# First token block of an MLP run in two halves around the whole second block, with x and a partial x2 kept in DRAM

## The chip, the cores and the metric

The kernel runs on one core of one Trainium2 chip. The metric is device time in microseconds (us) of one execution. A core has TensorE (PE; its weight loads are listed as PEld), VectorE (DVE), ScalarE (ACT), GpSimd (POOL) and the queues SP and POOL, from which transfers (DMA) are issued. Every engine and every queue works through its own instructions in a fixed order and waits on semaphores for the others.

## The reference

Three layers, all in float32, on 8 batches x 576 = 4608 tokens with 512 features:

```python
kv  = einsum('bhsd,bhse->bhde', k, v)            # linear attention, 8 heads of 64
out = einsum('bhsd,bhde->bhse', q, kv)
x   = out / sqrt(mean(out*out) + 1e-6) * g_norm  # laid out as 4608 x 512
h   = x @ w_in                                   # 512 -> 2048
x2  = (h * cos(h)) @ w_out                       # 2048 -> 512, the first MLP
out = (((x2 @ w1) * (x2 @ w2)) @ w3) @ w_out2    # the second MLP
```

## The kernel before

**Precision.** Every matmul operand is split into a high part (ACT, line 110) and a low part (`src - high`, line 112, on DVE or POOL). A product is three matmuls: high x high, high x low, low x high (`three`, line 501).

**Weights.** The weights come in as 8-byte words and are turned into float32 on the chip, chunk by chunk (`Chunk`, line 115). A chunk is 128 x 512 values: one load of 512 KB, one ACT operation (line 136), four DVE operations (lines 137, 138, 141, 144), and then `put`, which for the first MLP is one split: ACT 110 and DVE 112. The first MLP has 32 chunks: `i0` to `i15` for the 16 column blocks of w_in, `u0` to `u15` for the matching row blocks of w_out. Their order is i0, i1, i2, u0, i3, u1, ... i15, u13, u14, u15 (lines 223 to 229). Their words lie in buffers of w_out tiles that are not in use yet (tags `wo8` to `wo15`), and toward the end in the two `stage` buffers. 40 more chunks (w1, w2, w_out2, w3 of the second MLP) are converted one at a time during later blocks and written to DRAM.

**First MLP.** Tokens are cut into 9 blocks of 512, w_in into 16 column blocks, so there are 144 steps n; block t = n // 16 and column block m = n % 16. One step is `emit_h(n)` (12 matmuls of 128x512 into one of two banks `h`), then g = h * cos(h) (`g_first`, `g_rest`: four ACT and three DVE operations in the first block, one DVE operation more and one ACT operation less later on), and two steps behind `emit_w(n)` (12 matmuls into the four banks `acc`). So PE runs h_n, w_(n-2), h_(n+1), w_(n-1), ... At the first step of a block ("swap", line 883) w_(n-2) is put ahead of h_n, since the new x is split into the one buffer `x` (line 489) only after the old block's last h has read it. After the last w of a block the four `acc` banks are copied and stored to the DRAM tensor `x2_all` (lines 541 to 548).

**Conversion in the first block.** Before the loop 4 x 2 chunks are converted and put. Then each of steps 0 to 11 converts and puts two chunks (lines 891 to 893 and 902, 903). While `load["alone"]` holds (through step 15) all low parts go to DVE.

**Attention.** Attention is made in 16 units u of 288 tokens (batch u // 2, half u % 2). Units 0 and 1 are made before the loop. The others are `unit_stage(u, s)`, with stages s = 0 to 10: loads of k, v and q, kv matmuls, out matmuls, mean squares (s = 6), the Newton steps for the reciprocal root (s = 8, ten small DVE operations, one after the other), a round trip through DRAM that spreads it over partitions (`emit_bc`), and the multiplication `emit_x` (s = 10, line 385). Unit u starts at step `windows[u]`: units 2 and 3 at steps 2 and 4, units 4 and 5 at 15 and 20, units 6 and 7 at 31 and 36. Block 1 (tokens 512 to 1023) needs the end of unit 1 and units 2 and 3. Units 2 and 3 issue their DMAs from POOL, all others from SP. The unit's output `o_sb` has three buffers, k and v are loaded into the two `stage` buffers, the spread root into the one buffer `bc`.

**What sets the order.** The functions emit instructions in the order of the code; a scheduler with a simulated timeline then orders each engine's instructions, with the emission order as priority. So an instruction can run earlier than its place in the code where the simulation has a gap for it.

The second MLP follows the first and is not touched by the change.

Of the kernel before, what the change touches and what calls it, by code (L numbers as in the profile page):

```python
# [26 lines left out]
CHUNK = 512  # L27
# [7 lines left out]
def kernel(  # L35
# [18 lines left out]
    nc = tc.nc  # L54
    B, NPAIR, NHALF, _, HALF = qt.shape
# [5 lines left out]
    KD = DM // P  # L61
# [46 lines left out]
    def split(dst, src, lo_engine=None):  # L108

        nc.scalar.activation(dst[:, 0], src, AF.Copy)  # L110
        lo_engine = lo_engine or even(src.shape[-1])
        lo_engine.tensor_tensor(dst[:, 1], src, f32(dst[:, 0]), ALU.subtract)  # L112


    class Chunk:
# [5 lines left out]
        def load(self):  # L121
            if self.tag == "stage":
                self.words = stage([P, CHUNK, 2], I32, f"{self.name}_w")
            else:
# [53 lines left out]
    def put(count):  # L178
        for c in chunks[state["put"]:state["put"] + count]:
            c.put(c.f)  # L180
        state["put"] = min(len(chunks), state["put"] + count)
# [22 lines left out]
            w_out[m] = t  # L204
        return put

    spare = [f"wo{m}" for m in range(8, NM)]
    place = {}

    def add(name, src, put):  # L210
        place[name] = len(chunks) + 1
        chunks.append(Chunk(name, src, spare[0], put))
        spare.append(spare.pop(0))

    def add_pair(m, s):
        nm, put = (("i", put_w_in), ("u", put_w_out))[s]
        if s == 1 and f"wo{m}" in spare:
            spare.remove(f"wo{m}")
            if "stage" not in spare:
                spare.append("stage")  # L220
        add(f"{nm}{m}", w1pair[m, :, 2 * CHUNK * s:2 * CHUNK * (s + 1)], put(m))

    pairs = [(0, 0), (1, 0)]
    for m in range(2, NM):
        pairs += [(m, 0), (m - 2, 1)]
    pairs += [(NM - 2, 1), (NM - 1, 1)]
    for m, i in pairs:
        add_pair(m, i)
# [255 lines left out]
    x_hl = {}  # L484
    x2_d = dram.tile([P, KD, NT], F32, name="x2_all")

    def split_x(t, c, units=None):
        if t not in x_hl:
            x_hl[t] = m1.tile([P, 2, KD, TB], F32R, tag="x", name=f"x_{t}")
        done = 0  # L490
        while done < TB:
            u, s = divmod(t * TB + done, HALF)
            w = min(TB - done, HALF - s)
            if units is None or u in units:
                split(
                    x_hl[t][:, :, c, done:done + w], o_sb[u][:, c, s:s + w],
                    None if t == 0 else nc.vector,
                )
            done += w

    def three(ps, w, x, first, last):
        nc.tensor.matmul(ps, w[0], x[0], start=first, stop=False)  # L502
        nc.tensor.matmul(ps, w[0], x[1], start=False, stop=False)  # L503
        nc.tensor.matmul(ps, w[1], x[0], start=False, stop=last)  # L504

    def emit_h(n):
        t, m = divmod(n, NM)
        ps = ps_h.tile([P, 512], F32, tag="h", name=f"h_{n}")
        w, x = w_in[m], x_hl[t]
        for c in range(KD):  # L510
            three(ps, (w[:, 0, c], w[:, 1, c]), (x[:, 0, c], x[:, 1, c]), c == 0, c == KD - 1)
        h_ps[n] = ps

    def g_first(n):
        u, r = row(f"u_{n}"), row(f"r_{n}")
        nc.scalar.activation(u, h_ps[n], AF.Identity, bias=0.25, scale=INV_2PI)  # L516
        load["vector"] += 1600
        if n < NM:
            nc.scalar.activation(r, u, AF.Identity, bias=ROUND)
            nc.vector.scalar_tensor_tensor(u, r, ROUND, u, ALU.subtract, ALU.subtract)  # L520
        else:
            nc.vector.tensor_scalar(r, u, ROUND, ROUND, ALU.add, ALU.subtract)  # L522
            nc.vector.tensor_tensor(u, r, u, ALU.subtract)  # L523
        return u

    def g_rest(n, u):
        nc.scalar.activation(u, u, AF.Sin, scale=-TWO_PI_DOWN)  # L527
        nc.vector.tensor_tensor(u, u, h_ps.pop(n), ALU.mult)  # L528
        g = m1.tile([P, 2, TB], F32R, tag="g", bufs=2, name=f"g_{n}")
        split(g, u, None if n < NM else nc.vector)  # L530
        g_hl[n] = g

    def emit_w(n):
        t, m = divmod(n, NM)
        g = g_hl.pop(n)
        for j in range(KD):
            if m == 0:
                acc[j] = ps_acc.tile([P, 512], F32, tag=f"acc{j}", name=f"x2_{t}_{j}")
            w = w_out[m][:, :, j * P:(j + 1) * P]
            three(acc[j], (w[:, 0], w[:, 1]), (g[:, 0], g[:, 1]), m == 0, m == NM - 1)  # L540
        if m == NM - 1:
            for j in range(KD):
                s = row(f"x2s_{t}_{j}")
                if j % 2 == 0:
                    nc.scalar.activation(s, acc[j], AF.Copy)
                else:
                    nc.vector.tensor_copy(s, acc[j])
                nc.sync.dma_start(out=x2_d[:, j, t * TB:(t + 1) * TB], in_=s)

# [279 lines left out]
    if True:  # L829
# [39 lines left out]


        NS = NB * NM
        ready = 2
        windows = {}
        for t in range(NB - 1):
            need = min(NU, -(-(t + 2) * TB // HALF))
            new = list(range(ready, need))
            ready = need
            starts = ((2, 4) if t == 0 else (-1, 4)) if len(new) == 2 else (2,)
            for u, s in zip(new, starts):
                windows[u] = t * NM + s  # L880
        for n in range(NS + 2):
            t, m = divmod(n, NM)
            swap = m == 0 and 0 < n < NS
            if swap:
                emit_w(n - 2)
            stages = []
            if n == NM:
# [12 lines left out]
            run(stages, 2)  # L900
            if n < NS:
                if t == 0 and state["put"] < n_first:
                    put(2)
# [4 lines left out]
                if t + 1 < NB and m == NM - 1:  # L908
                    for c in range(2, KD):
                        split_x(t + 1, c)  # L910
            run(stages, 3)
            if 0 < t < NB - 1:
                if m % 2 == 1 and m >= 3 and state["conv"] > state["put"]:
                    put(1)
                if m % 2 == 1 and state["conv"] < state["load"]:
                    convert(1)
                if m % 2 == 1 and m < NM - 3:
                    prefetch(state["load"] + 1)
            if t == NB - 1:
# [178 lines left out]
```

## Time and profile before

| | us |
|---|---|
| three executions | 1854.87, 1558.01, 1563.22 |
| median of the three | 1563.22 |
| the profiled execution, its own time | 1560.76 |
| span of the profiled execution, first to last instruction | 1559.0 |
| PE busy | 1505.4 (97%) |
| DVE busy | 927.3 (59%) |
| ACT busy | 689.2 (44%) |
| POOL busy | 368.5 (24%) |

The span lacks what lies around the first and the last instruction: 1.76 us in this execution. The page divides the span into 40 slices of 39 us and gives each engine's busy share in tenths. A matmul's end is modelled and matmuls overlap, so a PE that is shown as busy need not be issuing at its full pace; the pace is read from the distance between the starts of successive matmuls, or of successive `u<-h` operations on ACT (line 516), each of which marks the end of one h_n.

### The profile page before, as it was taken

The page shows a single profiled execution, that of the slowest core. Times are in us where ns is not written, and L with a number is a line of the kernel's source. Part 1 is how long each engine was busy: PE and PEld are TensorE (multiplying, and loading weights), DVE is VectorE, ACT ScalarE, POOL GpSimd, SP SyncE. Part 2 cuts the span into 40 slices and gives each one's busy share as a digit, 9 for nine tenths or more (in the row PEclk, how much of TensorE's full clock was granted, in tenths as well). Part 3 has the DMA queues.
Part 4 walks back from the last instruction along what each step waited for, and adds up shares of the span by engine and source line. Part 5 has one row for each costly group of instructions (what it writes and reads, how often), then busy time and mean ns, then how long its engine had stood idle before and what let it go on. Part 6 is the DMA issues. An engine that isn't in the chain of part 4 may idle for free.

```text
span 1559.0 us, 20517 instructions
## 1 busy us (share of the span) xinstructions
PE 1505.4 (97%) x7616; PEld 1274.1 (82%) x7616; DVE 927.3 (59%) x1722; ACT 689.2 (44%) x1385; POOL 368.5 (24%) x301
## 2 busy tenths in 40 slices
PE   6778999999999999999999998999999999999998
PEld 5556787787787787877888787999999998998897
DVE  3999567566575666656665547745434456545453
ACT  4656544544445454444533335433333334333331
POOL 1100011011010111101102005464344317444420
PEclk9799999999999999999999999999999999999999
DMA  8633132332323424334112006121112313233312
GB/s 284 204 99 118 66 113 85 124 102 88 124 77 98 140 78 125 105 98 133 63 55 60 37 2 228 41 75 62 58 51 82 108 48 101 89 102 122 122 60 75
DMA packets 79748, 152.06 MB, mean 98 GB/s; under 512 B 11440, under 2 KB 36192, under 8 KB 79648
## 3 DMA queue, kind: packets, MB, share of 16 engines
q1 hardware_dynamic: 78032, 145.98, 28.8%
q0 software_dynamic: 1616, 4.78, 1.0%
q8 instruction: 59, 0.97, 0.2%
q14 instruction: 41, 0.34, 0.1%
HBM read 111.67 MB, written 39.06 MB: 97 GB/s over the span
## 4 chain that ended last, share of the span: by engine, by line
PE 80%; DVE 5%; DMA 5%; issue 4%; POOL 4%; ACT 2%; SPq 0%; ACTq 0%; POOLq 0%; DVEq 0%
PE X L732 11%; PE h L502 8%; PE h L503 8%; PE x L504 8%; PE h L504 8%; PE x L502 8%; PE x L503 8%; PE V L732 5%; PE o L502 4%; PE o L503 4%; PE o L504 4%; PE Y L732 2%; POOL xc L112 2%; DMA x2r<-x_all 2%; PE kv L271 2%
## 5 line engine op out<-in xcount | busy, mean ns | idle before, releaser
L502 PE MATMUL h<-x,w_in 128*128 128x512 f32 x576 | 230.7, 401 | 15.3 <-DVE u L528 14.1
L732 PE MATMUL X<-xc,w 128*128 128x384 f32 x1152 | 230.0, 337 | 7.9 <-ACT s L740 7.1
L503 PE MATMUL h<-x,w_in 128*128 128x512 f32 x576 | 229.2, 398 | 1.8 <-DVE x L112 1.8
L503 PE MATMUL x<-g,w_out 128*128 128x512 f32 x576 | 226.9, 394 | 2.0 <-DVE g L112 2.0
L504 PE MATMUL h<-x,w_in 128*128 128x512 f32 x576 | 228.0, 396 | 0.0
L504 PE MATMUL x<-g,w_out 128*128 128x512 f32 x576 | 227.4, 395 | 0.0
L732 PEld LDWEIGHTS X<-xc,w 128*128 128x128 f32 x1152 | 204.0, 188 | 21.2 <-ACT s L740 11.3
L502 PE MATMUL x<-g,w_out 128*128 128x512 f32 x576 | 213.3, 392 | 0.0
L112 POOL TENSOR_TENSOR xc<-x2r,xc 128x768 fp32r<-128x768 f32 x70 | 134.9, 1934 | 225.7 <-ACT xc L110 225.7
L516 ACT ACTIVATE u<-h 128x512 f32<-128x512 f32 x144 | 86.1, 598 | 172.9 <-PE h L504 163.9
L112 DVE TENSOR_TENSOR g<-u,g 128x512 fp32r<-128x512 f32 x144 | 107.8, 749 | 72.1 <-ACT g L110 71.9
L522 DVE TENSOR_SCALAR r<-u 128x512 f32<-128x512 f32 x128 | 57.9, 452 | 153.7 <-ACT u L516 153.7
L502 PEld LDWEIGHTS h<-x,w_in 128*128 128x128 f32 x576 | 109.5, 190 | 48.6 <-DVE u L528 22.9
L527 ACT ACTIVATE u<-u 128x512 f32<-128x512 f32 x144 | 91.0, 632 | 131.0 <-DVE u L523 123.5
L112 POOL TENSOR_TENSOR qhl<-q,qhl 128x288 fp32r<-128x288 f32 x48 | 40.2, 839 | 416.8 <-ACT qhl L110 415.8
L110 ACT ACTIVATE g<-u 128x512 fp32r<-128x512 f32 x144 | 90.9, 631 | 92.0 <-DVE u L528 73.7
L503 PEld LDWEIGHTS x<-g,w_out 128*128 128x128 f32 x576 | 108.7, 189 | 26.4 <-DVE g L112 2.4
L503 PEld LDWEIGHTS h<-x,w_in 128*128 128x128 f32 x576 | 109.6, 190 | 24.9 <-DVE x L112 2.5
L504 PEld LDWEIGHTS h<-x,w_in 128*128 128x128 f32 x576 | 109.6, 190 | 22.8
L504 PEld LDWEIGHTS x<-g,w_out 128*128 128x128 f32 x576 | 108.8, 189 | 23.4
L502 PEld LDWEIGHTS x<-g,w_out 128*128 128x128 f32 x576 | 107.8, 188 | 23.6
L528 DVE TENSOR_TENSOR u<-u,h 128x512 f32<-128x512 f32 x144 | 98.7, 686 | 47.1 <-ACT u L527 46.7
(174 smaller groups left out, 2535.2 us busy)
## 6 DMA issues: line engine op xcount, KB each, us to landing
x2r<-x_all SPq DMA_DIRECT2D x44, 384.0 KB, 3.5
kvraw<-in_kv_main_dram SPq DMA_DIRECT2D x28, 512.0 KB, 3.6
x_all<-x2s SPq DMA_DIRECT2D x36, 256.0 KB, 2.1
part<-o SPq DMA_DIRECT2D x36, 256.0 KB, 2.0
part<-part SPq DMA_DIRECT2D x36, 256.0 KB, 2.6
out_dram<-part SPq DMA_DIRECT2D x36, 256.0 KB, 2.8
i_w<-in_w1pair_dram SPq DMA_DIRECT2D x16, 512.0 KB, 5.6
u_w<-in_w1pair_dram SPq DMA_DIRECT2D x16, 512.0 KB, 4.0
```

The costliest lines, as they stand in the source:

```text
L110: nc.scalar.activation(dst[:, 0], src, AF.Copy)
L112: lo_engine.tensor_tensor(dst[:, 1], src, f32(dst[:, 0]), ALU.subtract)
L271: nc.tensor.matmul(ps[d, 0:D], k[:, d], v[:, d], start=i == 0, stop=i == NC)
L502: nc.tensor.matmul(ps, w[0], x[0], start=first, stop=False)
L503: nc.tensor.matmul(ps, w[0], x[1], start=False, stop=False)
L504: nc.tensor.matmul(ps, w[1], x[0], start=False, stop=last)
L516: nc.scalar.activation(u, h_ps[n], AF.Identity, bias=0.25, scale=INV_2PI)
L522: nc.vector.tensor_scalar(r, u, ROUND, ROUND, ALU.add, ALU.subtract)
L527: nc.scalar.activation(u, u, AF.Sin, scale=-TWO_PI_DOWN)
L528: nc.vector.tensor_tensor(u, u, h_ps.pop(n), ALU.mult)
L732: nc.tensor.matmul(ps, w[:, self.i, a, k], x[:, b, k], start=first and k == 0 and n == 0, stop=last and k == 1 and n == 2, skip_group_chec ...
```

## The change

The order of the steps is written out as a list `steps` of (t, m, first, last): first column blocks 0 to 7 of block 0 (n = 0 to 7), then all 16 of block 1 (n = 8 to 23), then column blocks 8 to 15 of block 0 (n = 24 to 31), then blocks 2 to 8 as before. Since block 0 is left and taken up again:

- `save_x0`: two DMAs on SP write units 0 and 1 as far as they belong to block 0 to DRAM ahead of the loop. `load_halves("x0")` at n = 20 loads them into the two `stage` buffers, and `split_x` splits them a second time at the end of step 23 (four splits of 128x512).
- After column block 7 of block 0 the four `acc` banks are copied and stored to a DRAM tensor `part0` (the same copies and stores as at a block's end). They are loaded at n = 28 into the `stage` buffers, and after n = 31's w they are added to the banks by four DVE operations, which take the place of two ACT and two DVE copies.
- There is one swap more: at n = 8, 24 and 32 instead of 16 and 32.
- The 32 first chunks are converted more slowly: at step n so many that 9 + n + min(n, 8) // 2 are done. That is 1, 1, 2, 1, 2, 1, 2, 1 in steps 0 to 7, 2 in step 8, 1 each in steps 9 to 19. The buffers of their words no longer include `stage`; the last chunk's words use the buffer `bc`.
- Units 2 and 3 are no longer placed by `windows`; the table `quick` puts their stages into steps 0 to 6: Newton of unit 2 in step 4, of unit 3 in step 5, `emit_x` in steps 5 and 6. Unit 6 starts at step 33 instead of 31.
- `load["alone"]` holds through step 23, the three-operation DVE form of g through step 31; the low part of g is always on DVE, as it was.
- The 40 later chunks are converted in steps 35 to 127, up to seven a block; before, steps 16 to 127, six a block.

The core of the diff:

```diff
+    HM = NM // 2
+    steps = [(0, m, m == 0, m == HM - 1) for m in range(HM)]
+    steps += [(1, m, m == 0, m == NM - 1) for m in range(NM)]
+    steps += [(0, m, m == HM, m == NM - 1) for m in range(HM, NM)]
+    steps += [(t, m, m == 0, m == NM - 1) for t in range(2, NB) for m in range(NM)]
+    x0_d = dram.tile([P, KD, TB], F32, name="x0")
+    part0_d = dram.tile([P, KD, TB], F32, name="part0")
+    halfway = {}
+    def save_x0():
+        for u in range(2):
+            w = min(HALF, TB - HALF * u)
+            nc.sync.dma_start(
+                out=x0_d[:, :, HALF * u:HALF * u + w], in_=o_sb[u][:, :, 0:w]
+            )
+    def load_halves(name, src):
+        halfway[name] = []
+        for i in range(2):
+            t = stage([P, 2, TB], F32, f"{name}_{i}")
+            nc.sync.dma_start(out=t, in_=src[:, 2 * i:2 * i + 2])
+            halfway[name] += [t[:, k] for k in range(2)]
     def split_x(t, c, units=None):
+        if "x0" in halfway and t == 0:
+            if c == 0:
+                x_hl[t] = m1.tile([P, 2, KD, TB], F32R, tag="x", name=f"x_{t}_again")
+            split(x_hl[t][:, :, c], halfway["x0"][c], nc.vector)
+            return
...
-        if m == NM - 1:
+        if last:
             for j in range(KD):
-                s = row(f"x2s_{t}_{j}")
-                if j % 2 == 0:
+                s = row(f"x2s_{n}_{j}")
+                if m == NM - 1 and t == 0:
+                    nc.vector.tensor_tensor(s, acc[j], halfway["part0"][j], ALU.add)
+                elif j % 2 == 0:
                     nc.scalar.activation(s, acc[j], AF.Copy)
                 else:
                     nc.vector.tensor_copy(s, acc[j])
-                nc.sync.dma_start(out=x2_d[:, j, t * TB:(t + 1) * TB], in_=s)
+                dst = part0_d[:, j] if m < NM - 1 else x2_d[:, j, t * TB:(t + 1) * TB]
+                nc.sync.dma_start(out=dst, in_=s)
...
-            starts = ((2, 4) if t == 0 else (-1, 4)) if len(new) == 2 else (2,)
+            starts = ((1, 4) if t == 2 else (-1, 4)) if len(new) == 2 else (2,)
...
+        quick = {
+            0: [(2, 0), (2, 1), (2, 2)], 1: [(2, 3), (2, 4), (3, 0), (3, 1)],
+            2: [(2, 5), (2, 6), (3, 2)], 3: [(3, 3), (3, 4)], 4: [(2, 8), (3, 5), (3, 6)],
+            5: [(2, 10), (3, 8)], 6: [(3, 10)],
+        }
+        save_x0()
         for n in range(NS + 2):
-            t, m = divmod(n, NM)
-            swap = m == 0 and 0 < n < NS
+            t, m, first, last = steps[n] if n < NS else (NB, n - NS, False, False)
+            swap = first and 0 < n
...
+            more = min(n_first, 9 + n + min(n, 8) // 2) - state["conv"] if n < NS else 0
...
-                if t == 0 and state["conv"] < n_first:
+                if more > 0:
                     prefetch(min(state["conv"] + 8, n_first))
-                    convert(2)
+                    convert(more)
...
-                if t + 1 < NB and m == NM - 1:
+                after = steps[n + 1][0] if last and n + 1 < NS else t
+                if after != t:
                     for c in range(2):
-                        split_x(t + 1, c)
+                        split_x(after, c)
...
+            for u, s in quick.get(n, ()):
+                one = [unit_stage(u, s)]
+                for i in range(4):
+                    run(one, i)
+            if n == NM + 4:
+                load_halves("x0", x0_d)
+            if n == 2 * NM - 4:
+                load_halves("part0", part0_d)
-            if 0 < t < NB - 1:
+            if 2 * NM + 2 < n < NS - NM:
```

## Rows read from the trace of the kernel before

**Rows 1.** The page: span, and busy tenths or granted clock in 40 slices.
```profile
span 1559.0 us, 20517 instructions
PE   6778999999999999999999998999999999999998
DVE  3999567566575666656665547745434456545453
PEclk9799999999999999999999999999999999999999
```
**Rows 2.** Stretches: length, each engine's busy us (count); then clock, DMA share, GB/s.
```profile
35.00:158.00 123.00, 99.93 (x514) 76.17 (x515) 115.79 (x256) 80.74 (x155) 11.21 (x18) 0.90 0.46 148
...
63.40:158.80 95.40, 77.56 (x335) 58.38 (x335) 87.93 (x189) 61.95 (x112) 9.05 (x14) 0.93 0.40 123
158.80:280.60 121.80, 121.80 (x584) 95.83 (x584) 74.79 (x155) 58.67 (x127) 14.68 (x16) 1.00 0.27 84
```
**Rows 3.** Timeline of ACT, chosen h_n ends: n = 0, 7, 8, 13, 33, 94, 95.
```profile
63.41 0.60 ACT L516 ACTIVATE u<-h 128x512 f32<-128x512 f32 x1 [0.85 <-PE h L504]
...
121.06 0.60 ACT L516 ACTIVATE u<-h 128x512 f32<-128x512 f32 x1
126.57 0.58 ACT L516 ACTIVATE u<-h 128x512 f32<-128x512 f32 x1
...
158.85 0.60 ACT L516 ACTIVATE u<-h 128x512 f32<-128x512 f32 x1 [1.21 <-PE h L504]
...
280.62 0.60 ACT L516 ACTIVATE u<-h 128x512 f32<-128x512 f32 x1 [1.21 <-PE h L504]
...
650.82 0.60 ACT L516 ACTIVATE u<-h 128x512 f32<-128x512 f32 x1 [1.58 <-PE h L504]
656.32 0.60 ACT L516 ACTIVATE u<-h 128x512 f32<-128x512 f32 x1 [0.98 <-PE h L504]
```
**Rows 4.** Waits of PE, 63.4 to 158.8 us: total, times, longest.
```profile
PE h L502 <- DVE u L528: 12.3, 9, 2.3
```
**Rows 5.** Timeline of DVE: one conversion's operations and g; two 288-wide operations.
```profile
141.75 0.70 DVE L141 SCALAR_TENSOR_TENSOR i_f<-i_w,i_f 128x512 int32<-128x512 int32 x1
142.35 0.43 DVE L138 TENSOR_SCALAR u_f<-u_f 128x512 int32<-128x512 int32 x1
142.69 0.70 DVE L112 TENSOR_TENSOR g<-u,g 128x512 fp32r<-128x512 f32 x1
143.29 0.70 DVE L144 SCALAR_TENSOR_TENSOR i_f<-i_w,i_f 128x512 int32<-128x512 int32 x1
...
50.98 0.45 DVE L112 TENSOR_TENSOR x<-o,x 128x288 fp32r<-128x288 f32 x1
51.34 0.68 DVE L112 TENSOR_TENSOR w_in<-i_f,w_in 128x512 fp32r<-128x512 f32 x1
```
**Rows 6.** DVE groups, 0 to 126.6 us, shapes apart: last conversion operation of each chunk.
```profile
L144 DVE SCALAR_TENSOR_TENSOR i_f<-i_w,i_f 128x512 int32<-128x512 int32 x13 | 8.9, 686 | 0.0
L144 DVE SCALAR_TENSOR_TENSOR u_f<-u_w,u_f 128x512 int32<-128x512 int32 x11 | 7.6, 687 | 0.0
```
**Rows 7.** Timeline of DVE: the low part of g_6.
```profile
121.81 0.70 DVE L112 TENSOR_TENSOR g<-u,g 128x512 fp32r<-128x512 f32 x1
```
**Rows 8.** Chain of waits, in time: kv matmuls of one head pair.
```profile
154.85 0.95 PE kv L271 x20
```
**Rows 9.** Timelines: unit 3's first and last Newton step, its bc transfers, its emit_x.
```profile
82.38 0.17 DVE L351 TENSOR_SCALAR rs<-rsx 128x18 int32<-128x18 int32 x1
...
101.14 0.18 DVE L357 SCALAR_TENSOR_TENSOR rs<-rs,rs 128x18 f32<-128x18 f32 x1
...
105.67 1.23 POOL L379 DMA_DIRECT2D bc<-rsd  x2 [3.49 <-DVE o L385]
...
110.77 1.19 DVE L385 TENSOR_TENSOR o<-o,bc 128x288 f32<-128x288 f32 x3 [0.51 <-DMA bc<-rsd]
...
113.08 0.45 DVE L385 TENSOR_TENSOR o<-o,bc 128x288 f32<-128x288 f32 x1
```
**Rows 10.** DMA issues: count, KB each, median us from issue to landing.
```profile
kvraw<-in_kv_main_dram SPq DMA_DIRECT2D x28, 512.0 KB, 3.6
x_all<-x2s SPq DMA_DIRECT2D x36, 256.0 KB, 2.1
```
**Rows 11.** Timeline of PE at half clock: two successive matmuls.
```profile
74.06 0.63 PE L502 MATMUL h<-x,w_in 128*128 128x512 f32 x1
74.48 0.63 PE L503 MATMUL h<-x,w_in 128*128 128x512 f32 x1
```

More of the change, by code (lines that the diff above doesn't have):

```diff
@@ L123, in load @@
                 self.words = stage([P, CHUNK, 2], I32, f"{self.name}_w")
+            elif self.tag == "bc":
+                self.words = ap.tile([P, CHUNK, 2], I32, tag="bc", name=f"{self.name}_w")
             else:
@@ L205, in put_w_out, with first_pairs @@
         return put
[L207 to L228, printed above, removed]
+    def first_pairs():
+        pairs = [(0, 0), (1, 0)]
+        for m in range(2, NM):
+            pairs += [(m, 0), (m - 2, 1)]
+        pairs += [(NM - 2, 1), (NM - 1, 1)]
+        free = list(range(NM // 2, NM))
+        for m, s in pairs:
+            if s == 1 and m in free:
+                free.remove(m)
+            tag = f"wo{free[0]}" if free else "bc"
+            free = free[1:] + free[:1]
+            nm, put = (("i", put_w_in), ("u", put_w_out))[s]
+            src = w1pair[m, :, 2 * CHUNK * s:2 * CHUNK * (s + 1)]
+            chunks.append(Chunk(f"{nm}{m}", src, tag, put(m)))
+    first_pairs()
     n_first = len(chunks)
@@ L506, in emit_h @@
     def emit_h(n):
-        t, m = divmod(n, NM)
+        t, m, _, _ = steps[n]
         ps = ps_h.tile([P, 512], F32, tag="h", name=f"h_{n}")
@@ L517, in g_first @@
         load["vector"] += 1600
-        if n < NM:
+        if n < 2 * NM:
             nc.scalar.activation(r, u, AF.Identity, bias=ROUND)
@@ L529, in g_rest @@
         g = m1.tile([P, 2, TB], F32R, tag="g", bufs=2, name=f"g_{n}")
-        split(g, u, None if n < NM else nc.vector)
+        split(g, u, nc.vector)
         g_hl[n] = g
     def emit_w(n):
-        t, m = divmod(n, NM)
+        t, m, first, last = steps[n]
         g = g_hl.pop(n)
         for j in range(KD):
-            if m == 0:
-                acc[j] = ps_acc.tile([P, 512], F32, tag=f"acc{j}", name=f"x2_{t}_{j}")
+            if first:
+                acc[j] = ps_acc.tile([P, 512], F32, tag=f"acc{j}", name=f"x2_{n}_{j}")
             w = w_out[m][:, :, j * P:(j + 1) * P]
-            three(acc[j], (w[:, 0], w[:, 1]), (g[:, 0], g[:, 1]), m == 0, m == NM - 1)
-        if m == NM - 1:
+            three(acc[j], (w[:, 0], w[:, 1]), (g[:, 0], g[:, 1]), first, last)
+        if last:
             for j in range(KD):
-                s = row(f"x2s_{t}_{j}")
-                if j % 2 == 0:
+                s = row(f"x2s_{n}_{j}")
+                if m == NM - 1 and t == 0:
+                    nc.vector.tensor_tensor(s, acc[j], halfway["part0"][j], ALU.add)
+                elif j % 2 == 0:
                     nc.scalar.activation(s, acc[j], AF.Copy)
@@ L871 @@
         NS = NB * NM
-        ready = 2
+        ready = 4
         windows = {}
-        for t in range(NB - 1):
+        for t in range(1, NB - 1):
             need = min(NU, -(-(t + 2) * TB // HALF))
@@ L886 @@
             stages = []
-            if n == NM:
+            if n == NM + HM:
                 load["alone"] = False
+            more = min(n_first, 9 + n + min(n, 8) // 2) - state["conv"] if n < NS else 0
             if n < NS:
                 stages = [unit_stage(u, n - w) for u, w in windows.items() if 0 <= n - w <= LAST]
-                if t == 0 and state["conv"] < n_first:
+                if more > 0:
                     prefetch(min(state["conv"] + 8, n_first))
-                    convert(2)
+                    convert(more)
                 emit_h(n)
@@ L901 @@
             if n < NS:
-                if t == 0 and state["put"] < n_first:
-                    put(2)
-                if t + 1 < NB and m == NM - 1:
+                if more > 0:
+                    put(more)
+                after = steps[n + 1][0] if last and n + 1 < NS else t
+                if after != t:
                     for c in range(2):
-                        split_x(t + 1, c)
+                        split_x(after, c)
                 g_rest(n, uu)
-                if t + 1 < NB and m == NM - 1:
+                if after != t:
                     for c in range(2, KD):
-                        split_x(t + 1, c)
+                        split_x(after, c)
             run(stages, 3)
-            if 0 < t < NB - 1:
+            for u, s in quick.get(n, ()):
[7 more added lines that the diff above has]
+            if 2 * NM + 2 < n < NS - NM:
                 if m % 2 == 1 and m >= 3 and state["conv"] > state["put"]:
@@ L916 @@
                     convert(1)
-                if m % 2 == 1 and m < NM - 3:
+                if m % 2 == 1 and m < NM - 2:
                     prefetch(state["load"] + 1)
+            if n == NS - NM:
+                assert state["put"] == len(chunks)
             if t == NB - 1:
```

1 line of the change is left out of this document (removed).

## The prediction

> **What bounds the kernel now.** The page comes first. PE is at nine tenths in nearly every slice but the first four, which hold the first 156 us; there DVE is the busiest engine and the granted clock dips [rows 1]. So the change can only win in the start, and the question is which engine sets the pace there. The stretches answer it: from 35 to 158 us DVE is busy for 115.8 of 123.0 us, PE for 99.9; from 158.8 to 280.6 us PE is busy for all of 121.8 us and DVE for 61% [rows 2]. The ends of the h matmuls date the change from one regime to the other. In the settled part a step takes 656.32 - 650.82 = 5.50 us, which is 24 matmuls at 0.229 us, or 2.75 us for one h or one w ("half-step"). From the end of h_13 at 158.85 to that of h_33 at 280.62 there are 20 steps in 121.77 us; 20 x 5.495 = 109.9, and the 11.9 us left are the matmuls of units 4 and 5, so nothing is lost after h_13. From h_0's end at 63.41 to h_13's at 158.85 PE did 13 h and 11 w, 24 half-steps, worth 65.9 us, in 95.4 us [rows 3]. With some 4 us of attention matmuls about 25 us are lost there. What PE waits for in that stretch is mostly DVE's product u * h, which frees the bank for the next h (12.3 us, 9 times) [rows 4].
>
> These 25 us are the ceiling of any gain. PE's idle time alone, 95.4 - 77.6 = 17.8 us [rows 2], would put it lower; I take the pace, since the matmuls shown as busy stand further apart there.
>
> The Trainium skill says the same in "Trainium Kernel Development and Optimization", section "Performance Expectations": matmul busy time is a bad metric because matmuls are pipelined, and the weight loads' busy share is a good one. The trace agrees: that share is 61% (58.4 of 95.4 us) against 79% (95.8 of 121.8 us) in the next stretch [rows 2]. By the busy rows the best case below would end near 1543 us instead of 1537.
>
> **What a conversion costs DVE.** By the distance of successive starts, an operation with two tensor inputs over 512 columns costs 0.60 us (141.75 to 142.35), one with a single input 0.34 us (142.35 to 142.69), one over 288 columns 0.36 us [rows 5]. A chunk is two of line 137/138, lines 141 and 144 and the low part of its split: 2 x 0.34 + 3 x 0.60 = 2.48 us. g costs three of 0.60, 1.80 us. So a step with two chunks wants 4.96 + 1.80 = 6.76 us of DVE and PE 5.50 us: DVE leads for the twelve converting steps. A step with one chunk wants 4.28 us and leaves PE in the lead.
>
> **Does DVE work in emission order?** By h_8's end at 126.57 us 13 + 11 = 24 chunks were converted [rows 3, 6]; the code has emitted 8 + 2 x 8 = 24 by the end of step 7. So conversions keep to the code's order, and I can count forward.
>
> **When h_8 ends after the change.** h_8 is now the first h of block 1. By the new schedule 19 chunks are done by the end of step 7, five fewer: 126.57 - 5 x 2.48 = 114.2 us. Added in front of it is the split of x for block 1: four column groups in pieces of 64, 288 and 160 columns, about 0.12 + 0.36 + 0.22 = 0.70 us a group (an estimate that runs a line through the 288 and 512 column prices), 2.8 us in all: 117.0 us. The other route is by w: the swap now puts w_6 ahead of h_8, and w_6 needs the low part of g_6, at 121.81 + 0.60 before [rows 7]. It stands behind the conversions of step 6, of which there are 18 instead of 22: 122.4 - 4 x 2.48 = 112.5 us, then w_6 and h_8, 5.5 us: 118.0 us. Both must hold, so I take 118.0. From below, PE's own pace bounds it: 63.41 plus 8 h and 7 w (41.2 us) plus some 3.5 us of units 2 and 3 is 108 us [rows 3].
>
> **What that is worth.** At 118.0 us PE has done 9 h and 7 w, 16 half-steps. Before, at 158.85 us, it had done 14 h and 11 w, 25, and two head pairs of unit 4, about 1.9 us at 0.95 each [rows 8]. If PE then runs at its pace it needs 9 x 2.75 + 1.9 = 26.6 us to get there: 144.6 instead of 158.85, a gain of **14.2 us**.
>
> **What goes off that.**
> - Step 8 still converts two chunks, and the first g in block 1 comes from a DVE that has no lead: 6.76 - 5.50, say 1.3 us lost. Steps 9 to 19 want 4.28 us of 5.50, so they hide.
> - Moved conversions (13 x 2.48 = 32 us of DVE) less the six later chunks that leave block 1 (11 us), plus four x splits, two copies and four adds (10 x 0.60) come to 27 us; DVE in that stretch goes from 74.8 to about 102 of 121.8 us [rows 2], 84%. Hidden behind PE; if that cover were gone each us would cost one.
> - The swap more: at the swaps at 16 and 32 PE has no idle time, since the whole stretch is busy [rows 2]. Nothing.
> - The DMAs: two saves, two loads of x, four stores and two loads of part0, all on SP. The nearest row has 2.1 us for a store of 256 KB, 3.6 for a load of 512 KB [rows 10]; issue at steps 20 and 28 leaves three and five steps (16 and 27 us). Hidden. The save of unit 0 holds its o buffer, which unit 3 wants, for a few us; the out matmuls of unit 3 come later than that. What waits behind part0 on `stage` is unit 6's first k and v load, 3.6 us, issued only when the adds are done; the kv matmuls that PE meets in the next step may wait. From 0 to 3 us; I take 1.0, since the scheduler can put the next w ahead of them.
> - Seven later chunks a block instead of six are 2.5 us of DVE in 96 us: nothing.
>
> 14.2 - 1.3 - 1.0 = 11.9. The profiled execution took 1560.76 us, 1.76 more than its span and 2.5 less than the median of the runs. 1560.8 - 11.9 = **1549 us**.
>
> **The rivals.**
> 1. *The gate moves to unit 3 (slower).* Before, units 2 and 3 were first wanted at h_16, far behind; now x of block 1 waits for them at h_8. Unit 3's Newton steps ran from 82.4 to 101.3 us, 19 us for ten operations of 0.17 us, since DVE puts others between them; then 9.5 us of round trips to the first emit_x at 110.8, the last ending at 113.5 [rows 9]. That is just in time for 118. But Newton is emitted in step 5, and if DVE takes it only when the step's other work is done (about 100 us; before, it ran far ahead of its place), the same 19 + 9.5 + 2.8 + 2.8 us lead to 134, and h_8 ends near 136. The price is 18 us, at half clock (0.43 us a matmul instead of 0.23 [rows 11]) up to 20: 1567 to 1569 us. It turns the sign when unit 3's last emit_x ends later than about 125 us. For it: every hop is a chain of waits. Against it: in the trace Newton ran well ahead of its place, and its priority is now higher. Chance 0.14.
> 2. *A smaller version, or DVE still leads in block 1.* The twelve x pieces have to fit behind h_7 (one x buffer) on a full DVE, and at 84% with static order some steps of block 1 can wait. Five to ten us go: h_8 near 125, or 1 us lost in each of eight steps. 1554 to 1560, about 1556 us. Chance 0.26.
> 3. *PE's own pace.* If the units' work fills gaps and clock dips go with the stalls, h_8 ends at 108 us, 10 us earlier, and nothing of the 2.3 us is lost: a gain of 24, 1537 us. For it: 5 chunks fewer also shorten PE's wait for banks. Against it: DVE stays full up to h_8. Chance 0.12.
>
> **How the numbers follow.** The forecast has 0.48, with its own range of 1542 to 1555 (h_8 between 112 and 122 us, deductions between 1 and 4 us). The range 1537 to 1562 takes in rival 2 and nearly all of rival 3; left out are most of rival 1 and a little beyond the ceiling, about 0.17. Two per cent of the median, 31 us, is about what a measurement of this kernel can tell from no change. The ceiling of 25 us lies inside it, so faster by more than that needs something that no row shows (0.03); slower by more needs rival 1 at nearly triple price (0.03); within it 0.94.
>
> **What would show it.** In the profile after: h_8's end near 118 us and PE without idle time from there (right), or h_8 late with the waits of its splits on unit 3's emit_x or bc (rival 1), or DVE over 95% busy up to 200 us with PE still waiting for u * h (rival 2). 19 conversions before h_8 shows that the emission order was kept. PE idle around h_24, h_32 or the first kv of unit 6 would show that the reloads are not hidden. The forecast is wrong at its root if the conversions run ahead of the new schedule again, since then DVE is as full before h_8 as it was.

## The result, and the profile after

The changed kernel takes 1546.2 us, median of five runs (1541.4 to 1548.3); the kernel before, run beside it, takes 1559.7. The ratio is 0.991, with a 95% interval of 0.988 to 0.994; one execution of the kernel before took 1854.9 us and is not in it. That is within 2%, 2.8 us under the 1549 forecast and inside the forecast's own range. (1.1 of these 2.8 us come from the base: the forecast started from 1560.8, the kernel before now has 1559.7.) The profiled execution has a span of 1544.4 us, 14.6 less than before [rows 1].

The page of the changed kernel: span, and busy tenths or granted clock in 40 slices.
```profile
span 1544.4 us, 20537 instructions
PE   6799999999999999999999998999999999999998
...
DVE  3998844566566666766666447644544456545453
...
PEclk9799999999999999999999999999999999999999
```
The kernel differs where the forecast looked for it: DVE is at eight tenths in slices 4 and 5 and at four in 6 and 7, where it was at nine, five, six and seven before. The ends of the h matmuls date the change. After, timeline of ACT: the ends of h_0, h_7, h_8, h_12, h_13 and h_33 (start, us; line 516 before is 543 now).
```profile
63.35 0.61 ACT L543 ACTIVATE u<-h 128x512 f32<-128x512 f32 x1
...
109.89 0.60 ACT L543 ACTIVATE u<-h 128x512 f32<-128x512 f32 x1
124.68 0.60 ACT L543 ACTIVATE u<-h 128x512 f32<-128x512 f32 x1 [1.36 <-PE h L531]
...
151.07 0.60 ACT L543 ACTIVATE u<-h 128x512 f32<-128x512 f32 x1 [0.37 <-PE h L531]
156.56 0.60 ACT L543 ACTIVATE u<-h 128x512 f32<-128x512 f32 x1 [1.16 <-PE h L531]
...
266.37 0.60 ACT L543 ACTIVATE u<-h 128x512 f32<-128x512 f32 x1 [0.29 <-PE h L531]
```
h_33 ends at 266.37 us instead of 280.62 [rows 3]: 14.25 us, so the whole gain is made by then. About 1.2 us of it are only moved: unit 6 starts two steps later. Before, 65 kv matmuls are shown from 158.85 to 280.62 us, 25 more than units 4 and 5 still had, and 25 x 0.95 / 20 = 1.2 us [rows 8]. h_143, far behind, ends at 920.51 instead of 933.80 us: 13.3. From h_12 on a step takes 5.49 us, (266.37 - 151.07) / 21, with nothing between: the matmuls of units 4 and 5, which stood after h_13 before, are already done. Stretches of the kernel after: length, busy us (count) of PE, PEld, DVE, ACT and POOL; then clock, DMA share, GB/s.
```profile
63.35:151.07 87.72, 79.75 (x389) 58.47 (x389) 76.68 (x177) 63.16 (x138) 16.83 (x21) 0.92 0.53 154
151.07:266.37 115.30, 115.30 (x505) 94.63 (x504) 71.50 (x133) 64.24 (x116) 7.45 (x8) 1.00 0.14 43
...
125.00:160.00 35.00, 33.97 (x158) 25.31 (x157) 30.60 (x67) 28.06 (x58) 5.71 (x6) 1.00 0.45 132
160.00:260.00 100.00, 100.00 (x439) 82.05 (x438) 59.76 (x106) 55.02 (x102) 7.45 (x8) 1.00 0.15 44
```
PE's idle time before the settled part is 87.72 - 79.75 = 8.0 us; before it was 17.8 [rows 2], so 9.9 us went there. Some 3 us more are matmuls that stand closer together: the work of PE's 77.6 us before [rows 2], with one step less (5.5) and units 4 and 5 more (11.9 - 1.2), would be 82.8 us, and 79.75 are shown. Of PE's wait for u * h, 12.3 us before [rows 4], 1.9 are left. After, waits of PE from 63 to 160 us (total, times, longest):
```profile
PE out L310 <- ACT qhl L110: 2.9, 1, 2.9
PE h L529 <- DVE u L555: 1.9, 3, 1.4
```

### The profile page after: what moved, and what is told of

Read it like the earlier page. It is cut to its first block, busy times and chain, and to the rows that moved or that the text cites. A ratio compares the mean times of both kernels' runs of the same rounds, so it can differ in the third digit from the quotient of the medians.

```text
span 1544.4 us, 20537 instructions
## 1 busy us (share of the span) xinstructions
PE 1500.9 (97%) x7616; PEld 1272.0 (82%) x7616; DVE 924.8 (60%) x1714; ACT 697.5 (45%) x1405; POOL 371.4 (24%) x301
## 4 chain that ended last, share of the span: by engine, by line
PE 81%; DMA 5%; DVE 3%; POOL 3%; ACT 2%; issue 2%; SPq 0%; ACTq 0%; POOLq 0%; DVEq 0%
PE X L762 11%; PE h L529 8%; PE x L531 8%; PE x L530 8%; PE h L531 8%; PE h L530 8%; PE x L529 8%; PE V L762 5%; PE o L529 4%; PE o L530 4%; PE o L531 4%; PE Y L762 3%; POOL xc L112 2%; DMA x2r<-x_all 2%; PE kv L269 1%
## 5 line engine op out<-in xcount | busy, mean ns | idle before, releaser
L529 PE MATMUL h<-x,w_in 128*128 128x512 f32 x544 | 216.3, 398 | 5.1 <-DVE u L555 3.4
L530 PE MATMUL h<-x,w_in 128*128 128x512 f32 x544 | 215.1, 395 | 1.8 <-DVE x L112 1.8
L531 PE MATMUL h<-x,w_in 128*128 128x512 f32 x544 | 215.0, 395 | 0.0
L554 ACT ACTIVATE u<-u 128x512 f32<-128x512 f32 x144 | 91.0, 632 | 121.6 <-DVE u L550 106.7
L112 DVE TENSOR_TENSOR g<-u,g 128x512 fp32r<-128x512 f32 x144 | 104.4, 725 | 64.6 <-ACT g L110 64.4
L110 ACT ACTIVATE g<-u 128x512 fp32r<-128x512 f32 x144 | 90.9, 632 | 109.1 <-DVE u L555 86.3
L529 PEld LDWEIGHTS h<-x,w_in 128*128 128x128 f32 x544 | 103.1, 190 | 33.0 <-DVE u L555 8.0
L531 PEld LDWEIGHTS x<-g,w_out 128*128 128x128 f32 x576 | 108.8, 189 | 23.0
L549 DVE TENSOR_SCALAR r<-u 128x512 f32<-128x512 f32 x112 | 50.7, 453 | 127.3 <-ACT u L543 127.2
L770 ACT ACTIVATE s<-X 128x384 f32<-128x384 f32 x144 | 65.9, 487 | 133.6 <-PE X L762 133.2
L530 PEld LDWEIGHTS h<-x,w_in 128*128 128x128 f32 x544 | 103.1, 190 | 24.4 <-DVE x L112 2.5
```

The lines of the kernel that those rows point to most:

```text
L770: nc.scalar.activation(s, ps, AF.Copy)
```

## The experiments

Three theories could give 14 us. **D**, the prediction's: fewer conversions before h_8 unload DVE, and the block order only makes that permissible. **G**: units 4 and 5 now run in PE's gaps before h_12. Their k and v load earlier, since the words of late chunks no longer take the `stage` buffers. **O**: the block order does something by itself. Later runs ask a second question: what holds h_8 at 124.7 us, the conversions or unit 3's chain. Runs on one chip are compared with each other; the ratio is to the kernel before on the same chip, with its 95% interval.

| run | median us | ratio (95%) | end of h_8 | end of h_33 |
|---|---|---|---|---|
| `stage` again for words | 1545.0 | 0.991 (0.990 to 0.993) | 120.7 | 266.5 |
| before, `stage` kept free | 1555.0 | 0.999 (0.998 to 1.000) | 125.5 | 278.6 |
| two chunks a step | 1558.6 | 1.001 (0.9995 to 1.002) | 130.9 | 276.7 |
| Newton first | 1546.9 | 0.993 (0.991 to 0.994) | 124.6 | 267.0 |
| one chunk a step | 1542.5 | 0.990 (0.989 to 0.992) | 117.1 | 260.4 |
| w_out's low parts on POOL | 1553.2 | 0.996 (0.995 to 0.998) | 133.5 | 273.1 |
| no clamp | 1547.1 | 0.993 (0.992 to 0.995) | 128.4 | 269.0 |
| one Newton round | 1547.8 | 0.993 (0.992 to 0.994) | 120.3 | 263.7 |
| no clamp, one Newton round | 1539.2 | 0.987 (0.985 to 0.989) | 117.8 | 259.1 |
| changed kernel again | 1546.0 | 0.992 (0.990 to 0.993) | 123.5 | 264.6 |
| one chunk a step again | 1541.7 | 0.989 (0.987 to 0.990) | 117.6 | 260.8 |

Rows 1 to 4 ran on one chip, 5 to 7 on a second and 8 to 11 on a third.

**Units 4 and 5 back in their place.** The changed kernel, with the words of late chunks in `stage` again:
```diff
                 free.remove(m)
-            tag = f"wo{free[0]}" if free else "bc"
+                if "stage" not in free:
+                    free.append("stage")
+            tag = free[0] if free[0] == "stage" else f"wo{free[0]}"
```


> The changed kernel with one part undone: words of the late first chunks go into the stage buffers again, as in the kernel before, instead of the buffer bc. In the program this moves the k/v matmuls of batch 2 (units 4 and 5) from steps 2 to 7 back to steps 14 to 20, and all out and mean-square matmuls of units 4 and 5 behind step 17; the conversion schedule and the order of the blocks stay. Theory G (the gain is units 4 and 5's matmuls done in PE's gaps of the first 150 us, let in by the free stage buffers): h_33 ends 8 to 12 us later than in the changed kernel (274 to 278 us), total 1553 to 1557 us. Theory D (the gain is the slower conversion, which frees DVE and brings h_8 forward): h_8 ends earlier or equal, total within 2 us of the changed kernel, 1544 to 1548 us.

The k and v matmuls of units 4 and 5 went back behind h_13, to steps 14 to 20. Stretches of this run, from h_0 to h_13, its part from h_8 on, and from h_13 to h_33, columns as above:
```profile
63.44:145.78 82.34, 74.15 (x294) 57.39 (x294) 75.31 (x168) 56.36 (x112) 8.59 (x13) 0.90 0.38 114
...
120.70:145.78 25.08, 25.08 (x111) 20.61 (x110) 23.23 (x44) 18.51 (x34) 0.00 (x0) 1.00 0.41 130
...
145.78:266.48 120.70, 120.70 (x599) 96.11 (x599) 71.43 (x142) 71.68 (x145) 13.52 (x16) 1.00 0.24 74
```
h_13 ends 10.8 us earlier than in the changed kernel, and the units' work then comes after it: h_33 ends at 266.48 against 266.37, and the time is the same. G falls. This run is also the prediction's own premise, units 4 and 5 behind block 1's first steps, so its terms are read from this run below.

**The same buffers in the kernel before.** Words never in `stage`, the last chunk's in `bc`:
```diff
...
             spare.remove(f"wo{m}")
-            if "stage" not in spare:
-                spare.append("stage")
+            if not spare:
+                spare.append("bc")
```


> The kernel before with one part of the change alone: the words of the first chunks never use the stage buffers, the last chunk's words use bc. Block order and conversion schedule are those of before. In the program the k/v matmuls of batch 2 now stand in steps 1 to 17 instead of 12 to 19, unit 5 stays behind step 22. Theory G: a part of unit 4's matmuls falls into the gaps, 2 to 5 us gained, 1555 to 1558 us. Theory D: no change within 1.5 us of the kernel before.

0.999, with an interval that just holds 1; the median is 2.3 us under that of the kernel before. The units' matmuls come earlier there too. By the interval they buy 0 to 3 us. That doesn't tell the two theories' numbers for this run apart, but it is far from 14.

**The new block order with the old conversions.** The changed kernel with two chunks in each of steps 0 to 11:
```diff
-            more = min(n_first, 9 + n + min(n, 8) // 2) - state["conv"] if n < NS else 0
+            more = min(n_first, 10 + 2 * n) - state["conv"] if n < NS else 0
```


> The changed kernel with the conversion schedule of before: two chunks in each of steps 0 to 11, so 24 instead of 19 before h_8. Units 4 and 5 stay in steps 2 to 10 in the program. Theory D: h_8 ends 5 x 2.48 = 12 us later (near 137 us) and steps 8 to 11 stay short of DVE time; total 8 to 12 us more, 1554 to 1558 us. Theory G: the same total of DVE work is done by step 20 either way, the gaps still take the units; total 0 to 4 us more, 1546 to 1550 us.

The whole gain goes: 1.001. h_7 ends at 120.8 us, as before (121.06 [rows 3]), and h_8 at 130.9. So O falls and D stands: the order of the blocks is worth nothing without the slower conversions.

The opposite half was not run: slower conversions in the old block order. By the order of the chunks, step n needs the first 2n of them. With 8 done ahead of the loop, 1.5 a step would be in time up to step 16 (8 + 1.5 x 16 = 32). By the prices of the prediction such a step wants 1.5 x 2.48 + 1.80 = 5.5 us of DVE, as much as PE takes; this is an estimate. So the runs show that the gain comes from the slower conversions; that it needs the new order of blocks as well they don't show.

**One chunk a step.** The other way on the same scale: 16 chunks by the end of step 7 instead of 19, one in each step but step 8 (two).
```diff
-            more = min(n_first, 9 + n + min(n, 8) // 2) - state["conv"] if n < NS else 0
+            more = min(n_first, 9 + n + (n >= 8)) - state["conv"] if n < NS else 0
```


> The changed kernel with a still slower conversion: one chunk a step (two in step 8), so 16 instead of 19 chunks before h_8, and the last in step 22 instead of 19. Theory D (DVE's conversions ahead of h_8 set its time): three chunks less are 7.4 us of DVE; h_8 near 117 instead of 124.7 us, steps 9 to 22 want 4.3 us of DVE and stay in PE's pace; total 4 to 7 us less than the changed kernel, 1539 to 1542 us. Theory T (only the sum of DVE work up to the end of the conversions counts, and it is the same): total within 1.5 us of the changed kernel.

Run again beside the changed kernel on one chip:

> The kernel with one chunk a step once more, beside the changed kernel on one chip. If fewer conversions ahead of h_8 are worth time: h_8 near 117 us again and the median 2 to 6 us under the changed kernel's. If only the sum of the work counts: within 1.5 us of it.

> The changed kernel once more, unchanged, for comparison on the same chip: ratio to the kernel before 0.990 to 0.992, h_8 within 3 us of 124.7 us.

1541.7 against 1546.0: 4.3 us, with intervals that don't touch. h_8 ends at 117.6 against 123.5, h_33 at 260.8 against 264.6. This version beats both kernels; its gain over before is 1.0% and 1.1% in the two runs.

**What holds h_8 at 124.7?** The timeline of DVE of the changed kernel from 112 us, some lines left out (start, us):
```profile
112.69 0.68 DVE L143 SCALAR_TENSOR_TENSOR i_f<-i_w,i_f 128x512 int32<-128x512 int32 x1
113.30 0.58 DVE L112 TENSOR_TENSOR x<-o,x 128x64 fp32r<-128x64 f32 x2
113.80 0.68 DVE L112 TENSOR_TENSOR w_out<-u_f,w_out 128x512 fp32r<-128x512 f32 x1
114.40 0.72 DVE L112 TENSOR_TENSOR x<-o,x 128x64 fp32r<-128x64 f32 x3
115.04 0.68 DVE L146 SCALAR_TENSOR_TENSOR i_f<-i_w,i_f 128x512 int32<-128x512 int32 x1
115.64 0.45 DVE L112 TENSOR_TENSOR x<-o,x 128x288 fp32r<-128x288 f32 x1
116.01 1.55 DVE L383 TENSOR_TENSOR o<-o,bc 128x288 f32<-128x288 f32 x4
117.49 0.68 DVE L112 TENSOR_TENSOR g<-u,g 128x512 fp32r<-128x512 f32 x1
...
120.24 1.02 DVE L112 TENSOR_TENSOR x<-o,x 128x160 fp32r<-128x160 f32 x4
```
The low part of g_6 (117.49), which w_6 needs, stands behind the 19th chunk, eight of x's pieces and unit 3's emit_x (116.01); x's last pieces, which h_8 needs, stand behind that emit_x too. DVE has no idle time in these lines, so the order alone doesn't tell which of the two gates, the amount of DVE work or unit 3's chain, holds h_8. The next runs take away one, the other, and both.

*Less DVE work:* line 139, the clamp, left out of the first chunks.
```diff
-            yield nc.vector.tensor_scalar(self.f, self.f, MOST, LEAST, ALU.min, ALU.max)
+            if not self.name[0] in "iu":
+                nc.vector.tensor_scalar(self.f, self.f, MOST, LEAST, ALU.min, ALU.max)
+            yield
```


> The changed kernel without the clamp (line 139 of the changed kernel, one DVE operation of 0.34 us a chunk) in the 32 first chunks; the values of these weights that lie outside the clamp's limits are left as they are. DVE does 32 x 0.34 = 10.9 us less, 6.5 us of it before h_8. If a microsecond of DVE work in the start is a microsecond of time: h_8 5 to 7 us earlier and total 6 to 10 us less, 1536 to 1540 us. If PE's order and its waits on the x splits set the time instead: under 3 us.

h_7 ends at 103.77 instead of 109.89: 6.1 us, which is 18 chunks by the 0.34 us of [rows 5] (5.1 us against the repeat of the changed kernel, where h_7 ends at 108.84). But the time is 0.993, no better than the changed kernel. Unit 3's emit_x starts at 117.01, 1 us later than in the changed kernel's profile, DVE now waits for its bc, and x's last pieces start at 120.20, where they did before. No clamp, timeline of DVE:
```profile
117.01 1.70 DVE L385 TENSOR_TENSOR o<-o,bc 128x288 f32<-128x288 f32 x4 [1.07 <-DMA bc<-rsd]
...
120.20 1.03 DVE L112 TENSOR_TENSOR x<-o,x 128x160 fp32r<-128x160 f32 x4
121.15 0.69 DVE L112 TENSOR_TENSOR w_in<-i_f,w_in 128x512 fp32r<-128x512 f32 x1
129.69 0.69 DVE L549 SCALAR_TENSOR_TENSOR u<-r,u 128x512 f32<-128x512 f32 x1 [7.86 <-ACT r L548]
```
DVE then stands idle for 7.9 us: the time won is waited away. (h_8 is listed later, at 128.4, since h_9's matmuls ran among its own; h_9 ends at 130.1 here and at 130.8 in the changed kernel.)

*A shorter chain:* one Newton round instead of three for units 2 and 3.
```diff
...
-        newton(x, y, t)
+        newton(x, y, t, 1 if u in (2, 3) else 3)
```


> The changed kernel with one Newton iteration instead of three in units 2 and 3 (six of the ten small DVE operations left out; the reciprocal roots of these 576 tokens are coarser). Giving Newton priority had not shortened it (86 to 105 us still), so this takes the operations away: unit 3's chain should be some 10 us shorter, its emit_x end near 106 instead of 117.6 us. If unit 3's chain is the gate of h_8 in the changed kernel: h_8 near 118 instead of 124.7 us and the total 4 to 6 us under the repeat of the changed kernel. If DVE's conversions are the gate: h_8 moves by under 2 us and the total by under 2 us.

The first operation of emit_x in this run, timeline of DVE:
```profile
106.50 0.83 DVE L383 TENSOR_TENSOR o<-o,bc 128x288 f32<-128x288 f32 x2 [3.12 <-DMA bc<-rsd]
```
It starts 8.4 us earlier than in the changed kernel's repeat on this chip (114.86), and h_8 ends at 120.3 instead of 123.5. Only 0.9 us of that is left at h_33, and the time is 1547.8 against 1546.0: no gain.

*Both:*

> The changed kernel without the clamp in the 32 first chunks and with one Newton iteration instead of three in units 2 and 3. Without the clamp alone h_7 ended 6.1 us earlier (103.8), as 18 x 0.34 us of DVE less would have it, but h_8 ended at 128.4 us, since unit 3's emit_x came at 117.0 to 118.7 us. If that run's h_8 was held by unit 3's chain: emit_x now ends near 107 us, h_8 near 116 us, total 6 to 10 us under the changed kernel's repeat. If h_8 is held by something else (PE's order, the x buffer): h_8 stays above 123 us and the total within 3 us of it.

1539.2 against 1546.0: 6.8 us. emit_x of unit 3 and h_8 in this run (timelines of DVE and ACT):
```profile
108.86 1.55 DVE L385 TENSOR_TENSOR o<-o,bc 128x288 f32<-128x288 f32 x4
...
117.78 0.60 ACT L545 ACTIVATE u<-h 128x512 f32<-128x512 f32 x1 [0.94 <-PE h L533]
```
Either gate alone is worth nothing and the two together 6.8 us, as two gates that stand side by side would have it.

One rival is not taken apart from this: the granted clock differs too. Stretches of this run and then of the changed kernel's repeat, columns as above:
```profile
45.00:80.00 35.00, 31.40 (x169) 23.02 (x166) 29.45 (x65) 25.34 (x59) 5.52 (x10) 1.00 0.63 199
...
45.00:80.00 35.00, 25.35 (x122) 16.54 (x119) 30.40 (x73) 23.36 (x53) 6.50 (x9) 0.76 0.62 199
```
All five executions of the run with both show a mean granted clock of 0.996 to 0.999 over the whole span, those of the repeat 0.992, so a part of the 6.8 us can be the clock's. Two things speak against its being the whole: h_0 ends 2.4 us earlier here (59.6 against 62.0), but h_7 at 108.4 against 108.8, so that little of the early lead is left there; and the run with one chunk a step, which relieves both gates too, gains 4.3 us with the same 0.76 from 45 to 80 us.

Two gates also fit what one chunk a step gains. It takes three chunks (7.4 us) out of DVE before h_8 and, with fewer conversions between the Newton steps, lets unit 3's Newton take its last step at 93.9 us instead of 105.5. One chunk a step, the run repeated, timeline of DVE:
```profile
93.91 0.17 DVE L355 SCALAR_TENSOR_TENSOR rs<-rs,rs 128x18 f32<-128x18 f32 x1
105.52 1.56 DVE L383 TENSOR_TENSOR o<-o,bc 128x288 f32<-128x288 f32 x4 [4.00 <-DMA bc<-rsd]
```

**Newton first.** The chain shortened without leaving anything out, by priority:
```diff
-            late.append(lambda: emit_newton(u))
+            late.append(lambda: newton_first(u))
...
+    def newton_first(u):
+        with tc.high_priority() if u in (2, 3) else nullcontext():
+            emit_newton(u)
```


> The changed kernel with one wait shortened: the ten Newton steps of units 2 and 3 get priority over all other DVE work, so that they follow each other. In the changed kernel unit 3's took 21 us (86 to 107 us) and its emit_x ended at 117.6 us, with h_8 at 124.7. If unit 3's chain is the gate of h_8: emit_x ends near 100 us, h_8 near 118 us, total 4 to 6 us less, 1540 to 1542 us. If DVE's work as a whole is the gate: h_8 moves by under 2 us and the total by under 1.5 us.

It didn't do what it was made for: unit 3's Newton still ran from 86.0 to 104.3 us (86.3 to 106.4 in the changed kernel), and the time is unchanged. Its emit_x did start 3.5 us earlier, at 112.55 us instead of 116.01, with h_8 where it was (124.6): a chain that is a little shorter alone is worth nothing. The run with one Newton round shows the same with a larger step.

**w_out's low parts on POOL.** DVE relieved in another way, by six operations of 0.60 us between h_0 and h_8:
```diff
-            split(t, f)
+            split(t, f, nc.gpsimd)
             w_out[m] = t
```


> The changed kernel with the low parts of the 16 w_out chunks on POOL instead of DVE: 16 x 0.60 = 9.6 us of DVE less in the first 20 steps, some 7 of them (4.2 us) before h_8. Theory D and theory T both: h_8 3 to 5 us earlier, total 3 to 8 us less, 1538 to 1543 us. If the two engines hinder each other, the DVE operations beside POOL's get longer than 0.69 us and the gain is under 2 us.

It loses more than half of the gain: 1553.2 us against 1557.9 before on this chip, and h_8 ends at 133.5. Timeline of POOL in this run (start, us, in brackets the idle time before and what ended it):
```profile
86.49 1.41 POOL L377 DMA_DIRECT2D bc<-rsd  x2 [2.60 <-DMA rsd<-rs]
87.97 1.22 POOL L343 DMA_DIRECT2D msd<-ms_sb  x2
94.19 0.58 POOL L344 DMA_DIRECT2D rsx<-msd  x1 [5.01 <-DMA msd<-ms_sb]
...
110.06 2.06 POOL L112 TENSOR_TENSOR w_out<-u_f,w_out 128x512 fp32r<-128x512 f32 x1 [5.95 <-ACT w_out L110]
113.60 0.58 POOL L373 DMA_DIRECT2D rsd<-rs  x1 [1.48 <-DVE rs L355]
```
Unit 3's msd is issued at 87.97 (78.56 in the changed kernel), now behind unit 2's bc, and w_out's operations stand between the chain's transfers. The chain starts 9.4 us later and its emit_x 5.6 us later (121.56 against 116.01); x's last pieces, behind it, start at 126.29 instead of 120.24, and h_8's matmuls come after these. Some operations of DVE got longer as well (last section); how much of the loss is theirs was not tried by itself.

Not tried: a second x buffer, which would take the splits of block 1 out of the stretch behind h_7. Whether there is room for it beside the weights no run shows.

## Why the prediction was right, step by step

**The mechanism was right.** The gain is the conversions' schedule, by the experiments on either side of it, all in the new block order. 11.9 us were forecast; the medians show 13.6, the end of h_143 13.3.

**The price of a chunk held.** The clamp's 0.34 us, by 18 chunks, moved h_7 by 5.1 to 6.1 us, where the sum gives 6.1; the exact agreement is in part luck, since h_7 itself ends 1.05 us apart in two executions of the changed kernel.

**Emission order held.** 19 chunks were converted by h_8's end, as counted from the schedule. After, groups of DVE up to 124.6 us: the last conversion operation of each chunk.
```profile
L146 DVE SCALAR_TENSOR_TENSOR i_f<-i_w,i_f 128x512 int32<-128x512 int32 x11 | 7.5, 680 | 0.0
...
L146 DVE SCALAR_TENSOR_TENSOR u_f<-u_w,u_f 128x512 int32<-128x512 int32 x8 | 5.5, 684 | 0.0
```

**h_8 at 118.0 was too early; this term was mis-sized, in two parts.** Under the prediction's premise, the run with `stage` again, the route over g_6's low part comes out nearly to the letter: done at 112.5 forecast, 112.90 measured, behind 18 conversions. That run, timelines of DVE and of PE, and a stretch with its clock (columns as above):
```profile
112.30 0.67 DVE L112 TENSOR_TENSOR g<-u,g 128x512 fp32r<-128x512 f32 x1
112.90 1.55 DVE L385 TENSOR_TENSOR o<-o,bc 128x288 f32<-128x288 f32 x4
...
110.15 1.21 PE L531 MATMUL x<-g,w_out 128*128 128x512 f32 x4 [1.49 <-ACT g L110]
113.02 0.80 PE L532 MATMUL x<-g,w_out 128*128 128x512 f32 x1 [1.67 <-DVE g L112]
...
118.31 0.63 PE L532 MATMUL h<-x,w_in 128*128 128x512 f32 x1
118.74 0.49 PE L533 MATMUL h<-x,w_in 128*128 128x512 f32 x1
119.06 0.39 PE L531 MATMUL h<-x,w_in 128*128 128x512 f32 x1
119.29 0.39 PE L532 MATMUL h<-x,w_in 128*128 128x512 f32 x1
...
113.00:119.00 6.00, 5.98 (x14) 4.72 (x15) 6.00 (x16) 3.03 (x8) 0.00 (x0) 0.51 0.00 0
```
But w_6 and h_8 were then put at full speed, 5.5 us. PE had just waited twice (1.5 and 1.7 us), and the 14 matmuls from 113.02 to 119.06 stand 0.43 us apart, as in [rows 11]: the granted clock is 0.51 there, the lower level of 1.2 GHz. From 119 to 125 us it is 1.00 and they stand 0.23 apart. 14 x 0.2 = 2.8 us, and h_8 is 2.7 late, at 120.70. (Four of w_6's matmuls had run earlier, at 110.15; their 0.9 us about make up for the 0.4 us by which the low part was late and what lies between the last matmul and the mark on ACT.) The prediction had the row for half speed and used it in a rival only.

The other 4.0 us, to 124.68, belong to the shift that wasn't foreseen. In the changed kernel the kv matmuls of units 4 and 5 all stand before h_8, and all of their work before h_12. g_6's low part starts at 117.49, 5.2 us later than in the run above, behind one conversion more (2.48), unit 3's emit_x (116.01 to 117.49, 1.5) and some low parts of kv. So h_8 is later there, what follows is shorter, and the total is the same.

**From h_8 on it went better than forecast.** DVE didn't lead in step 8: with `stage` again PE is busy for all of the 25.08 us from h_8 to h_13, nine half-steps at 2.75 and 0.3 more. So h_13's 145.78, where the sum has 144.6 + 1.3 = 145.9, is in part luck: h_8 is 2.7 late, the 1.3 us aren't lost, and the two head pairs of unit 4 (1.9 us) come only later. In the changed kernel PE is busy for all of 151 to 266 us with DVE at 62%; from 125 to 160 us DVE has 87% (84% had been worked out for block 1) and PE 97%. Rival 2 was wrong that DVE would still lead there, though it had named twelve pieces of x on a full DVE rightly.

**The hidden costs were hidden.** PE has no idle time around h_24 and h_32, where x and part0 come back and the extra swap stands (the whole of 151 to 266 us is busy). The 1.0 us that had been taken for unit 6's load was not lost either: its first kv matmuls stand at 277.25 us without a wait, and PE is busy throughout. After, a stretch, columns as above:
```profile
260.00:300.00 40.00, 40.00 (x241) 32.16 (x240) 22.27 (x43) 18.22 (x39) 2.43 (x3) 1.00 0.38 126
```

**Rival 1's mechanism was there, not its price.** Unit 3's emit_x ended at 117.6 us, 4 later than before, and not past the 125 from which it would have turned the sign. Newton ran ahead of its place again. But it is a second gate: with the conversions lightened alone (no clamp) x's last pieces still wait for it, and in the run on POOL, where it started at 121.6, more than half of the gain was gone. Rival 3, PE's own pace with h_8 at 108 us, is far off: the nearest run had 117.1.

**The ceiling was the pace, not PE's idle time.** Of the gain, 9.9 us were idle time and some 3 closer matmuls, the share that idle time doesn't show. About 12 us of the 25 are left; the run with both gates lightened takes 6.8 of them, and its 19.5 us over the kernel before (1558.7 on that chip) are more than the 17.8 us of idle time.

What stays open: the terms don't close to the last microsecond. With h_8 2.7 us late, and the 1.3 us of step 8 and the 1.0 us of unit 6 not lost, the forecast gain of 11.9 becomes 11.5; measured are 13.3 to 13.6, some 2 us more. With `stage` again, 10.9 us beyond the 20 steps lie between h_13 and h_33, where before 11.9 + 1.9 - 1.2 = 12.6 would be wanted for the same work; that is 1.7 of the 2 us, and why it is less isn't known. Why the low part of g_6 is placed behind x's pieces and emit_x on DVE is read from the order and was not tried by itself. Executions of one kernel differ by 2 to 7 us, so that the run with one Newton round (h_33 0.9 us earlier, median 1.9 us later) can't be told from no change.

## What to carry to other kernels

Work that must be done "by some step" should be spread out as late as its users allow; here reordering the blocks was worth nothing with the old conversions and gave them later due times; whether slower conversions would have paid without it was not run. When one engine is full ahead of a switch, look for a second chain that ends at the same moment before judging a relief: two gates side by side make each of them look worthless when it is taken away alone. Look at the granted clock in every stretch in which TensorE waits, in two runs that are compared as well, and carry the half-clock price as a term of its own. A wait alone doesn't tell: with `stage` again half clock followed the waits of 1.5 and 1.7 us at 110 and 113 us, but in the kernel before this wait of 1.9 us was followed by matmuls 0.23 us apart, at a granted clock of 1.00 from 100 to 106 us (timeline of PE):
```profile
101.29 0.50 PE L502 MATMUL h<-x,w_in 128*128 128x512 f32 x1 [1.94 <-DVE u L528]
```

## What the runs showed that was not expected

- Ten operations of 0.17 us on 128x18 elements took 20 us on a full DVE (86.3 to 106.4 us), and raised priority left them at 18 us (86.0 to 104.3); three chunks fewer on DVE brought them to 10.6 (83.3 to 93.9).
- The low part of a w_out chunk, 0.60 us on DVE, took 1.29 to 2.58 us on POOL, and several operations of DVE lengthened in that run. Groups of DVE with w_out's low parts on POOL, 63 to 125 us; the same two groups have a mean of 684 and 680 ns in the changed kernel:
```profile
L112 DVE TENSOR_TENSOR w_in<-i_f,w_in 128x512 fp32r<-128x512 f32 x6 | 5.0, 838 | 0.7 <-ACT w_in L110 0.7
...
L146 DVE SCALAR_TENSOR_TENSOR i_f<-i_w,i_f 128x512 int32<-128x512 int32 x5 | 4.8, 959 | 0.0
```
